# A decode kernel on one core: a hand-written program that closes its Tile context early, with its first load inside it, batch rows 16 partitions apart, and one DMA each for x and the output

## Chip, cores, metric

One core of a Trainium2 chip. The metric is the device time of one execution in microseconds (us). A profile gives the *span*, from the first to the last instruction of the program; the measured time is up to 1.9 us longer than the span. Clocks are the mean granted TensorE clock, as a share of full speed.

In the profiles PE is TensorE (matmuls), PEld its weight loads, DVE VectorE, ACT ScalarE, POOL GpSimd; SPq, ACTq and PEq are the instruction queues of SyncE, ScalarE and PE. A semaphore is a counter that one engine or DMA raises and another waits for. At an all-engine barrier every engine waits for all others. The Tile context is the scope in which the program is built; leaving it adds such barriers and instructions that the trace calls drains. wq, wo, w3 and w4 are weights; sg is the product of the attention branch and the gate.

## The reference

Grouped-query attention for one new token against a long cache, gated by a small MLP branch:

```python
B, Sq, D = 2, 1, 512;  Hq, Hkv, Sk, Dh = 32, 8, 32768, 128       # bf16
xn = layernorm(x)
q  = (xn @ wq)                                   # 32 heads; 4 heads share one K/V head
p  = softmax(q @ k_cache^T * Dh**-0.5);  o = p @ v_cache
s  = o @ wo
g  = silu(mlp_branch(xn, w3, w4))                # at S=1 the w1/w2 branch adds zero
return x + s * g
```

K and V are 2 x 8 x 32768 x 128 bf16 each, 268 MB together. Everything else is small.

## The kernel before

It is written by hand inside one `tc.tile_critical()`, with its own semaphores. SyncE issues all large loads in one queue, K and V of the 16 (batch, head) groups alternately; DVE transposes K, PE multiplies, ScalarE takes the exponential, PE multiplies by V. After the last group 128 short matmuls apply wo.

```python
with tc.tile_critical():
    ...
    k_wq = d_wq.after(sp.dma_start(out=wq_t[...], in_=A_wq...), 16)      # first load of the program
    k_w3 = ...;  k_w4 = ...;  load_k(0)
    ...
    for n in range(NQ):                                                  # x, four DMAs of two rows
        k_x = d_x.after(act.dma_start(out=x_bf[32*n:32*n+B, :], in_=A_x[:, 0, :]), 16)
    ...                                                                  # layernorms, q, the MLP branch
    wait(sp, k_h2)                                                       # frees the buffer of w3, w4
    load_v(0)
    for m in range(1, NG):
        sp.wait_ge(p_k, m);  load_k(m)
        sp.wait_ge(p_o, m);  load_v(m)
    for i, (g0, g1, c0, c1) in enumerate(WO_PARTS):                      # wo in 8 parts, last in the queue
        d_wo[i].after(sp.dma_start(out=wo3[...], in_=wos[...]), 16)
    ...
    with pe.Fori(0, NG): ...                                             # the 16 groups
    pe.wait_ge(s_r, NG)                                                  # last group's result
    for i, (g0, g1, c0, c1) in enumerate(WO_PARTS):
        wait(pe, (d_wo[i], 16))
        ...  pe.matmul(s_ps[32*n:32*n+B, :], lhsT=oXv[:, g, r, :], rhs=wo3[...])   # 128 in all
    ...                                                                  # two DVE operations: sg, out4
    for b, eng in ((0, sp), (1, act)):
        wait(eng, k)
        d_o[b].after(eng.dma_start(out=out[b, 0, :]..., in_=out4[b:QP:32, :]), 16)
    for b, eng in ((0, sp), (1, act)):
        wait(eng, (d_o[b], 16))
# leaving the context adds drains, two all-engine barriers and a clearing of semaphores
```

The softmax here doesn't subtract the row's maximum and nothing guards it: scores larger than these inputs give would overflow.

Of the kernel before, what the change touches and what calls it, by code (L numbers as in the profile page):

```python
# [7 lines left out]
F32 = mybir.dt.float32  # L8
BF16 = mybir.dt.bfloat16
I32 = mybir.dt.int32  # L10
# [5 lines left out]
RT = 16  # L16
VT = 4
T_BUFS = 4
PAD = 384
# [18 lines left out]
def wait(eng, *marks):  # L38
    for count, n in marks:
        if n > 0:  # L40
            eng.wait_ge(count.sem, n)
# [8 lines left out]
def kernel(  # L50
# [14 lines left out]
    nc = tc.nc  # L65
    pe, dve, act, pool, sp = nc.tensor, nc.vector, nc.scalar, nc.gpsimd, nc.sync
# [10 lines left out]
    NPART = 2  # L77
# [8 lines left out]
    QW = D // NQ  # L86
    QP = 32 * (NQ - 1) + B
    NU = KPT // VT
# [4 lines left out]

    pers = ctx.enter_context(tc.tile_pool(name="pers", bufs=1))
    psum = ctx.enter_context(tc.tile_pool(name="psum", bufs=1, space=bass.MemoryType.PSUM))

    pers.tile([128, PAD // 4], F32, name="pad")
    kbuf = pers.tile([128, 3 * SLOT], BF16, name="kbuf")
    vbuf = pers.tile([128, 2 * SLOT], BF16, name="vbuf")
    Ts = [pers.tile([128, RT * NB * 32], I32, name=f"T{i}") for i in range(T_BUFS)]  # L100
    eps_ = [pers.tile([128, RT * 32], BF16, name=f"ep{i}") for i in range(NPART)]
    pts = [pers.tile([128, NR, RT * rep], BF16, name=f"pt{i}") for i in range(NPART)]
    rss = [pers.tile([128, 1], F32, name=f"rs{i}") for i in range(NPART)]
    sms = [pers.tile([128, rep], F32, name=f"sm{i}") for i in range(NPART)]
    z = pers.tile([128, NB, 2, ZC], BF16, name="z")
    ob = pers.tile([128, VT * Dh], F32, name="ob")
    rec = pers.tile([128, rep], F32, name="rec")
    on = pers.tile([128, rep], BF16, name="on")
    xm = pers.tile([128, NQ, rep], F32, name="xm")
    oX = pers.tile([128, B * Hkv * NQ], BF16, name="oX")  # L110
    ident = pers.tile([128, 128], BF16, name="ident")
    ones_f = pers.tile([128, 128], F32, name="ones_f")
    sel = pers.tile([128, NB, 2, 4, 32], BF16, name="sel")
    sel_o = pers.tile([128, VT, rep], F32, name="sel_o")
    sel_h = pers.tile([128, rep], F32, name="sel_h")
    sel_r = pers.tile([128, NQ, 4, 32], BF16, name="sel_r")
    mask = pers.tile([128, NQ, rep], F32, name="mask")
    x_bf = pers.tile([128, D], BF16, name="x_bf")
    xf = pers.tile([128, D], F32, name="xf")
    xn = pers.tile([128, D], F32, name="xn")  # L120
    ln2 = pers.tile([128, D], F32, name="ln2")
    xn_bf = pers.tile([128, D], BF16, name="xn_bf")
    ln2_bf = pers.tile([128, D], BF16, name="ln2_bf")
    x4 = pers.tile([128, QW], F32, name="x4")
    xn4 = pers.tile([128, QW], F32, name="xn4")
    xT = pers.tile([128, 2 * DK, B], BF16, name="xT")
    q_sb = pers.tile([128, B, Hq], BF16, name="q_sb")
    qr = pers.tile([128, NB, 2, B * Hq], BF16, name="qr")
    hf = pers.tile([128, FK * B], F32, name="hf")
    x2 = pers.tile([128, FK * B], F32, name="x2")  # L130
    inner = pers.tile([128, FK * B], F32, name="inner")
    th = pers.tile([128, FK * B], F32, name="th")
    h_bf = pers.tile([128, FK * B], BF16, name="h_bf")
    t_f = pers.tile([128, QW], F32, name="t_f")
    sig = pers.tile([128, QW], F32, name="sig")
    g4 = pers.tile([128, QW], F32, name="g4")
    sg = pers.tile([128, QW], F32, name="sg")
    out4 = pers.tile([128, QW], BF16, name="out4")
    stats = [pers.tile([128, dve.BN_STATS_DIM], F32, name=f"stats{i}") for i in range(2)]
    mv = [pers.tile([128, dve.BN_AGGR_DIM], F32, name=f"mv{i}") for i in range(2)]  # L140
    rstd = [pers.tile([128, 1], F32, name=f"rstd{i}") for i in range(2)]

    banks = [psum.tile([128, 512], F32, name=f"bank{i}") for i in range(8)]
    sc = banks[0:2]
# [3 lines left out]
    xp = xp_b[:, 0:NQ * rep].rearrange("p (r h) -> p r h", h=rep)  # L148
    treg = treg_b[:, 0:DK * B].bitcast(BF16)
    qT_ps = sc[0][:, 0:Hq * B]  # L150
# [8 lines left out]

    with tc.tile_critical():  # L160
        d_x, d_wq, d_w3, d_w4 = (Count(nc, n) for n in ("d_x", "d_wq", "d_w3", "d_w4"))
        s_k = [nc.alloc_semaphore(f"s_k{i}") for i in range(NPART)]
        s_v = [nc.alloc_semaphore(f"s_v{i}") for i in range(NPART)]
        d_wo = [Count(nc, f"d_wo{i}") for i in range(len(WO_PARTS))]
        d_o = [Count(nc, f"d_o{i}") for i in range(B)]
        v_, p_, a_, g_ = (Count(nc, n) for n in ("v_", "p_", "a_", "g_"))
# [6 lines left out]
        def V(inst):  # L173
            return v_.after(inst)

        def P(inst):
            return p_.after(inst)
# [10 lines left out]

        wq_t = kbuf[:, 2 * SLOT:3 * SLOT]
        w34 = vbuf[:, 0:SLOT]  # L190
        wo3 = kbuf[:, 0:Hq * D].rearrange("p (g c) -> p g c", g=Hkv)

        k_wq = d_wq.after(sp.dma_start(out=wq_t[:, 0:DK * HD], in_=A_wq.rearrange("(p k) f -> p (k f)", k=DK)), 16)
        k_w3 = d_w3.after(sp.dma_start(out=w34[:, 0:W4O], in_=B_w3.rearrange("(p k) f -> p (k f)", k=DK)), 16)
# [25 lines left out]
        wait(act, k_x0)  # L220
        for n in range(NQ):
            k_x = d_x.after(act.dma_start(out=x_bf[32 * n:32 * n + B, :], in_=A_x[:, 0, :]), 16)

# [13 lines left out]
        V(dve.memset(o[:, :], 0.0))  # L237
        V(dve.memset(s_ps, 0.0))
        k_h0 = V(dve.memset(h2, 0.0))

# [23 lines left out]
        wait(dve, k_xn)  # L264
        k_xb = V(dve.tensor_copy(out=xn_bf[0:B, :], in_=xn[0:B, :]))
        k_l2 = layernorm(1, ln2, xn, k_xn)
        wait(dve, k_l2)
        k_lb = V(dve.tensor_copy(out=ln2_bf[0:B, :], in_=ln2[0:B, :]))

        wait(pool, k_n0, k_xn)  # L270
        for n in range(NQ):
            r0, r1, c0, c1 = 32 * n, 32 * n + B, n * QW, (n + 1) * QW
            wait(pool, (g_, g_.n))
            k = G(pool.tensor_copy(out=x4[r0:r1, :], in_=xf[r0:r1, c0:c1]))  # L274
            wait(pool, k)
            k_x4 = G(pool.tensor_copy(out=xn4[r0:r1, :], in_=xn[r0:r1, c0:c1]))

        wait(pe, k_id)
        for s, (src, k_src) in enumerate(((xn_bf, k_xb), (ln2_bf, k_lb))):
            wait(pe, k_src)  # L280
            for k in range(DK):
                c = (s * DK + k) * B
                k_tr = P(pe.transpose(out=treg[:, c:c + B], in_=src[0:B, k::DK], identity=ident[0:B, 0:B]))  # L283

# [27 lines left out]
        wait(dve, k_tr)  # L312
        k_xT = V(dve.tensor_copy(out=xT[:, :, :], in_=treg.rearrange("p (k b) -> p k b", b=B)))

        wq3 = wq_t[:, 0:DK * HD].rearrange("p (k f) -> p k f", k=DK)
        wait(pe, k_xT, k_wq)
        for h in range(Hq):
# [53 lines left out]
        wait(dve, k)  # L371
        k_hb = V(dve.tensor_mul(out=h_bf[:, :], in0=hf[:, :], in1=th[:, :]))
        wait(pe, k_h0, k_hb, k_w4)
        for f in range(FK):
            for n in range(NQ):
                i = pe.matmul(
                    h2[32 * n:32 * n + B, :], lhsT=h_bf[:, f * B:(f + 1) * B],
                    rhs=w4v[:, f, n * QW:(n + 1) * QW],
                    start=(f == 0), stop=(f == FK - 1), tile_position=(0, 32 * n),
                )  # L380
# [137 lines left out]

        oXv = oX[:, :].rearrange("p (b g r) -> p g r b", b=B, g=Hkv)
        pe.wait_ge(s_r, NG)  # L520
        for i, (g0, g1, c0, c1) in enumerate(WO_PARTS):
            wait(pe, (d_wo[i], 16))
            for g in range(g0, g1):
                for r in range(c0 // D, c1 // D):
                    for n in range(NQ):
                        c = r * D + n * QW
                        mm = pe.matmul(  # L527
                            s_ps[32 * n:32 * n + B, :], lhsT=oXv[:, g, r, :], rhs=wo3[:, g, c:c + QW],
                            start=(g == 0 and r == 0), stop=(g == Hkv - 1 and r == NQ - 1),
                            tile_position=(0, 32 * n),  # L530
                        )
# [4 lines left out]
        k = V(dve.tensor_tensor(out=out4[0:QP, :], in0=sg[0:QP, :], in1=x4[0:QP, :], op=ALU.add))  # L536
        for b, eng in ((0, sp), (1, act)):
            wait(eng, k)
            d_o[b].after(
                eng.dma_start(out=out[b, 0, :].rearrange("(n c) -> n c", c=QW), in_=out4[b:QP:32, :]), 16  # L540
            )
        for b, eng in ((0, sp), (1, act)):
            wait(eng, (d_o[b], 16))

# [29 lines left out]
```

## Time and profile before

657.5 us, median of three runs (657.25 to 657.61); span 655.9 us, clock 0.82.

| of the span | |
|---|---|
| start: first instruction to the first load packet | 1.98 us |
| stream: first load packet to the end of the last wo packet | 649.42 us |
| last wo packet to the first of the two last DVE operations | 0.61 us |
| those two, to the issue of the output DMA | 0.65 us |
| output issued by SyncE to its landing seen by SyncE | 1.95 us |
| from there to the last instruction (closing the context) | 1.29 us |

The rows come from the starts and ends of the trace's instructions and DMA packets and add up to the span. The page of the kernel before: parts 1 and 2 (busy time; the span in 40 slices, busy share in tenths) and the sum of part 3.

```profile
span 655.9 us, 7180 instructions
PE 391.5 (60%) x2716; PEld 168.8 (26%) x2748; DVE 337.2 (51%) x428; ACT 71.3 (11%) x167; POOL 5.6 (1%) x18
...
DMA  8999999999999999999999999999999999999996
...
q1 hardware_dynamic: 6744, 280.50, 99.0%
...
HBM read 280.50 MB, written 0.00 MB: 428 GB/s over the span
```

The DMA row is what to read: 90% or more in every slice but the first and the last. The SyncE queue (q1) carries the bytes and is never empty between its first and last packet. PE and DVE have slack; a time saved on them in the middle is worth nothing. What can be won without moving fewer bytes is the start and the tail.

The timeline of the kernel before, start and end (start us, duration us, engine, line, operation, tiles; in brackets the idle time before and what ended it; SPq and ACTq lines are DMA issues):

```profile
0.96 0.40 SPq L193 DMA_DIRECT2D kbuf<-in_A_wq_dram  x1
...
1.37 1.57 ACTq L222 DMA_DIRECT2D x_bf<-in_A_x_dram  x4
1.42 0.41 SPq L194 DMA_DIRECT2D vbuf<-in_B_w_dram  x1
...
13.53 0.43 DVE L242 CAST xf<-x_bf 128x512 f32<-128x512 bf16 x1 [11.31 <-DMA x_bf<-in_A_x_dram]
...
21.37 3.58 PE L319 MATMUL bank<-xT,kbuf 128*128 128x2 bf16 x128 [2.00 <-DVE xT L313]
...
32.40 0.33 SPq L202 DMA_DIRECT2D vbuf<-in_A_v_cache_dram  x1
...
641.77 1.90 PE L495 MATMUL bank<-vbuf,pt 128*16 128x512 bf16 x32 [1.89 <-PEq L46]
...
651.10 0.86 PE L527 MATMUL bank<-kbuf,oX 128*2 128x128 bf16 x16 [0.31 <-DMA kbuf<-in_A_wo_dram]
...
652.01 0.29 DVE L534 TENSOR_TENSOR sg<-bank,g 98x128 f32<-98x128 f32 x1 [4.69 <-PE bank L527]
652.34 0.29 DVE L536 TENSOR_TENSOR out<-sg,x 98x128 bf16<-98x128 f32 x1
652.65 0.66 SPq L540 DMA_DIRECT2D out_dram<-out  x1
652.66 0.60 ACTq L540 DMA_DIRECT2D out_dram<-out  x1
```

The first V load is issued at 32.40 us, while K of the first group keeps the queue busy to 42.1 us: the x chain in front of it has slack. At the end the wo matmuls wait for the last wo DMA, so the tail here is the DMA's. The span ends at 655.9 us, 3.2 us after the output is issued. The list of waits of the SyncE queue (who waited for what: us in total, times, longest) shows how much of this is the output's landing (1.3 us after its issue is over); the rest is the close:

```profile
SPq L160 <- DMA out_dram<-out: 1.3, 1, 1.3
SPq L558 <- PEq L558: 0.7, 1, 0.7
SPq L569 <- PEq L569: 0.5, 2, 0.4
```

### The profile page before, as it was taken

The numbers are of one execution on the slowest core, as the hardware profiler recorded it, in microseconds if no ns is written. First come the engines' busy times: TensorE is split into PE (matmuls) and PEld (weight loads), VectorE is DVE, ScalarE is ACT, GpSimd is POOL, SyncE is SP. The second block draws the span as 40 slices with busy tenths as digits, with TensorE's granted clock in tenths as the row PEclk, the third lists the DMA queues.
The fourth block names the chain that finished last, engine by engine and source line by source line (L and its number), as shares of the span: only waits on it lengthen the run. The fifth ranks groups of instructions, "written<-read, shape, count | busy, mean of one in ns | idle before, by whom it ended". The sixth has DMA issues, their size and how long they took to land. (4 is left out here: it accounts for less than half of the span.)

```text
span 655.9 us, 7180 instructions
## 1 busy us (share of the span) xinstructions
PE 391.5 (60%) x2716; PEld 168.8 (26%) x2748; DVE 337.2 (51%) x428; ACT 71.3 (11%) x167; POOL 5.6 (1%) x18
## 2 busy tenths in 40 slices
PE   0528295582838648293764829376382946728784
PEld 0513132221313223131331313223131322313323
DVE  2348092653809265290835629084471917448560
ACT  0110102001010200101020010202001020200100
POOL 1200000000000000000000000000000000000000
PEclk9999787686978868698786978779597876959898
DMA  8999999999999999999999999999999999999996
GB/s 365 436 441 448 441 408 440 440 444 440 404 440 444 444 420 428 440 444 444 400 448 440 444 444 400 448 436 448 440 404 444 440 444 416 432 440 418 444 420 263
DMA packets 6774, 280.59 MB, mean 428 GB/s; under 512 B 744, under 2 KB 1008, under 8 KB 2032
## 3 DMA queue, kind: packets, MB, share of 16 engines
q1 hardware_dynamic: 6744, 280.50, 99.0%
q8 instruction: 4, 0.07, 0.0%
q14 instruction: 2, 0.02, 0.0%
q10 hardware_dynamic: 24, 0.01, 0.0%
HBM read 280.50 MB, written 0.00 MB: 428 GB/s over the span
## 5 line engine op out<-in xcount | busy, mean ns | idle before, releaser
L477 PE MATMUL bank<-T,z 128*128 128x512 bf16 x992 | 274.2, 425 | 178.5 <-PEq L46 174.5
L434 DVE STREAM_TRANSPOSE T<-kbuf 128x1024 int32<-128x1024 int32 x256 | 290.9, 1206 | 131.2 <-DVEq L46 130.6
L477 PEld LDWEIGHTS bank<-T,z 128*128 128x128 bf16 x1024 | 98.4, 104 | 340.1 <-issue 262.5
L495 PE MATMUL bank<-vbuf,pt 128*16 128x512 bf16 x1024 | 73.2, 449 | 1.9 <-PEq L46 1.9
L413 ACT ACTIVATE ep<-bank 128x512 bf16<-128x512 f32 x32 | 19.1, 597 | 440.3 <-ACTq L46 440.3
L447 DVE RECIPROCAL rec<-bank 128x4 f32<-128x4 f32 x16 | 2.9, 182 | 118.2 <-DVEq L46 118.2
L495 PEld LDWEIGHTS bank<-vbuf,pt 128*16 128x16 bf16 x1024 | 27.8, 102 | 39.5 <-issue 21.7
L441 DVE STREAM_TRANSPOSE pt<-ep 128x512 bf16<-128x512 bf16 x32 | 22.1, 691 | 23.4 <-DVEq L46 23.4
L488 PE MATMUL bank<-sm,ones_f 128*128 128x4 f32 x64 | 9.3, 251 | 29.3 <-PEq L46 29.3
L506 PE MATMUL bank<-sel_o,ob 128*128 128x4 f32 x128 | 16.4, 252 | 13.8 <-PEq L46 13.8
L417 ACT COPY ob<-bank 128x512 f32<-128x512 f32 x16 | 9.4, 586 | 103.2 <-ACTq L46 103.2
L406 ACT ACT_TABLE_LOAD x16 | 20.5, 1283 | 0.3
L506 PEld LDWEIGHTS bank<-sel_o,ob 128*128 128x128 f32 x128 | 15.5, 191 | 18.2 <-issue 18.2
L488 PEld LDWEIGHTS bank<-sm,ones_f 128*128 128x128 f32 x64 | 8.3, 190 | 30.2 <-issue 30.2
L406 ACT COPY z<-qr 32x16 bf16 x64 | 12.9, 201 | 0.7
L512 PE MATMUL bank<-on,sel_r 128*128 128x4 bf16 x64 | 3.9, 165 | 12.6 <-PEq L46 12.6
L283 PE MATMUL bank<-ident,xn_bf 2*128 2x2 bf16 x4 | 0.3, 165 | 16.7 <-POOL x L274 16.7
L464 PE MATMUL bank<-ident 128*1 128x1 bf16 x64 | 8.3, 164 | 0.0
L464 PEld LDWEIGHTS bank<-ident 128*1 128x1 bf16 x64 | 4.0, 81 | 16.0 <-issue 14.2
L450 DVE TENSOR_TENSOR xm<-bank,mask 128x16 f32<-128x16 f32 x16 | 2.8, 174 | 8.6 <-DVEq L46 8.6
L512 PEld LDWEIGHTS bank<-on,sel_r 128*128 128x128 bf16 x64 | 2.9, 98 | 13.5 <-issue 13.5
L413 ACT ACTIVATION_READ_ACCUMULATOR ep<-bank 128x1 f32 x32 | 6.3, 198 | 0.2
(66 smaller groups left out, 58.8 us busy)
## 6 DMA issues: line engine op xcount, KB each, us to landing
kbuf<-in_A_k_cache_dram SPq DMA_DIRECT2D x2, 4096.0 KB, 22.7
vbuf<-in_A_v_cache_dram SPq DMA_DIRECT2D x2, 4096.0 KB, 25.6
kbuf<-in_A_wq_dram SPq DMA_DIRECT2D x1, 4096.0 KB, 12.2
vbuf<-in_B_w_dram SPq DMA_DIRECT2D x2, 1792.0 KB, 17.9
kbuf<-in_A_wo_dram SPq DMA_DIRECT2D x2, 1024.0 KB, 33.3
kbuf<-in_A_wo_dram SPq DMA_DIRECT2D x3, 512.0 KB, 35.7
kbuf<-in_A_wo_dram SPq DMA_DIRECT2D x1, 256.0 KB, 26.8
kbuf<-in_A_wo_dram SPq DMA_DIRECT2D x2, 128.0 KB, 15.6
```

Source lines behind the costliest of these rows:

```text
L406: i = act.copy(out=z[32 * j:32 * j + 32, :, :, c:c + rep], in_=qr[32 * j:32 * j + 32, :, :, bass.ds(m * rep, rep)],)
L413: act.activation(out=eps_[i][:, :], in_=sc[i][:, :], func=ACT.Exp, scale=inv_sqrt_dh, accum_out=rss[i][:, :]).then_inc(s_e, 1)
L417: act.copy(out=ob[:, :], in_=o[:, :]).then_inc(s_ob, 1)
L434: dve.transpose(out=Ts[(NR * i + r) % T_BUFS][:, :].rearrange("p (b t k) -> p t b k", b=NB, t=RT), in_=kt[:, r * W:(r + 1) * W].rearrange( ...
L441: dve.transpose(out=pts[h][:, :, :].rearrange("p r (t h) -> p t r h", h=rep), in_=eps_[i][:, :].rearrange("p (t r h) -> p t r h", r=NR, h= ...
L447: then(dve.reciprocal(out=rec[:, :], in_=S))
L464: pe.matmul(mark_ps, lhsT=ident[:, 0:1], rhs=ident[:, 0:1], start=True, stop=True).then_inc(sem, 1)
L477: mm = pe.matmul(sc[i][:, :], lhsT=z[:, nb, e, zc:zc + 128], rhs=Tb[:, nb, :, e], start=(r == 0 and nb == 0 and e == 0), stop=(r == NR - 1 ...
L488: pe.matmul(S, lhsT=ones_f[:, :], rhs=sms[h][:, :], start=(h == 0), stop=(h == NPART - 1))
L495: mm = pe.matmul(o[32 * j:32 * j + VT * rep, :], lhsT=pts[h][:, r, a * VT * rep:(a + 1) * VT * rep], rhs=vt[:, u * VT:(u + 1) * VT, :].rea ...
L506: mm = pe.matmul(oT, lhsT=ob[:, t * Dh:(t + 1) * Dh], rhs=sel_o[:, t, :], start=(t == 0), stop=(t == VT - 1))
L512: mm = pe.matmul(xp[:, r, :], lhsT=sel_r[:, r, :, :].rearrange("p j w -> p (j w)"), rhs=on[:, :], start=True, stop=True,)
```

## The change

The intent is to cut what the context adds at both ends: the buffers come from raw allocations, the context contains nothing but the first load (wq) and is closed before the rest of the program is written, so its barriers run behind wq's packets and nothing but one wait follows the output. And x and the output, four and two small DMAs, become one each: batch rows lie 16 partitions apart instead of next to each other, so that one regular pattern with step 16 reaches all eight (quarter, batch) rows. The price is 17 columns of PE weights for 2 and DVE operations on 113 rows for 98.

```diff
-    pers = ctx.enter_context(tc.tile_pool(name="pers", bufs=1))
-    kbuf = pers.tile([128, 3 * SLOT], BF16, name="kbuf")
+    kbuf = sbuf([128, 3 * SLOT], BF16, "kbuf")          # nc.alloc_sbuf_tensor; the same for all buffers
...
-    with tc.tile_critical():
+    first = sp.dma_start(out=wq_t[:, 0:DK * HD], in_=A_wq.rearrange("(p k) f -> p (k f)", k=DK))
+    first.then_inc(s_wq, 16)
+    tc.no_tile_sem_insts.add(first.ins.name)
+    tc.close()
+    tc.compile()
...
-        for n in range(NQ):
-            k_x = d_x.after(act.dma_start(out=x_bf[32 * n:32 * n + B, :], in_=A_x[:, 0, :]), 16)
+        k_x = d_x.after(act.dma_start(out=x_bf[0:QP:BS, :],
+                  in_=A_x[:, 0, :].unsqueeze(0).to_broadcast([NQ, B, D])), 16)      # BS = 16
...
-                            s_ps[32 * n:32 * n + B, :], lhsT=oXv[:, g, r, :], rhs=wo3[:, g, c:c + QW],
+                            s_ps[32 * n:32 * n + BW, :],                            # BW = 17
+                            lhsT=oX[:, g * NQ + r:g * NQ + r + BO + 1:BO // BS], rhs=wo3[:, g, c:c + QW],
...
-        for b, eng in ((0, sp), (1, act)):
-            d_o[b].after(eng.dma_start(out=out[b, 0, :]..., in_=out4[b:QP:32, :]), 16)
-        for b, eng in ((0, sp), (1, act)):
-            wait(eng, (d_o[b], 16))
+        sp.dma_start(out=out[:, 0, :].rearrange("b (n c) -> n b c", c=QW), in_=out4[0:QP:BS, :]
+        ).then_inc(s_out, 16)
+    sp.wait_ge(s_out, 16)
```

## The prediction

> **What bounds the kernel now.** The stream of loads. In the page's slices the 16 DMA engines are 90% busy or more from the second slice to the second last; 280.5 MB move at 428 GB/s. From the trace's DMA packets: the SyncE queue's first load packet starts at 1.98 us, the last wo packet ends at 651.40 us, and in between the queue is never empty. In the timeline each K and V load is issued some 7 to 12 us before the one ahead of it has landed. So PE (60% busy) and DVE (51%) have slack, and the time is 2.0 us of start + 649.4 us of stream + 4.5 us of tail.
>
> **What the change does.**
>
> 1. *Start.* Before, SyncE leaves the first barrier at 0.65 us, runs a NOP and a waiting branch, and issues wq at 0.96 us. After, wq is its first instruction: about 0.72 us, so the stream starts 0.24 us earlier. Two barriers now come after that issue. From those at the end of the old trace (about 0.4 us each), the w3 load, the memsets and the x load begin 0.3 to 0.8 us later: hidden behind wq's 10 us of packets.
>
> 2. *x load.* Four DMAs become one. In the old trace ScalarE's packets take turns with 32 KB packets of wq, one each 1.22 us per engine: four DMAs, each a data packet and a semaphore packet, last from 6.3 to 13.2 us. The Trainium skill ("DMA: Bandwidth & Descriptors", "Why a DMA increments its semaphore by 16 and not by 1") tells how many engines a copy uses: two for two rows (the trace agrees: two data packets a DMA), four for the new shape, so two data packets and one semaphore packet each. Estimate: x lands at 9 to 10 us instead of 13.2, the q matmuls start near 17 us (21.4), the first V load is issued near 28 us (32.4). Worth nothing: K0 keeps the queue busy to 42 us.
>
> 3. *Stream.* The same bytes, packet sizes and buffer addresses (compared in the two builds). PE weights of 17 columns for 2 and DVE operations on more rows cost the same by free size. Change 0 +-0.3 us.
>
> 4. *Tail.* After the last wo packet: four matmuls, two DVE operations (0.29 us each), output DMA. The two output DMAs are seen at 654.34 (ScalarE) and 654.61 us (SyncE). One DMA saves 0 to 0.25 us. Then the old kernel closes the context: drains, NOP, two barriers, a clearing of semaphores, from 654.61 to 655.90 us, all after the result has landed. After, a single wait ends it. Saves 1.25 us.
>
> On the critical path: 0.24 + 0.1 + 1.25 = 1.6 us. x load: nothing.
>
> **Prediction:** 655.9 us, 80% range 655.1 to 656.9 us. Chances: faster by over 2% 0.005, within 2% 0.99, slower 0.005.
>
> **What would show it.** Timeline: wq issued near 0.7 us; wait of xf for x ends at 9 to 10 us; first V load near 28 us; no gap in the SyncE queue, loads spaced 19.3 us; the last instruction near 654.3 us, under 0.2 us after the output DMA's semaphore.
>
> **What would make it wrong.** SyncE's drain after the wq issue waits until wq has landed: then w3 is issued near 13 us and the queue has a gap of 2 us (time near 657.7 us). Or the measured time holds parts outside the span (657.8 against 655.9 us in the profiled run) that grow as the barriers go. Or the stream's rate shifts by 0.2%.

## The result and the profile after

655.38 us (median of four runs, 655.07 to 656.12) against 657.39 us (four runs): ratio 0.9971, 95% interval 0.9954 to 0.9988. Ratios here are the mean time of one kernel's runs over that of the other's of the same rounds, so not quite the ratio of the quoted medians. That is 2.0 us less by the medians: clear of noise, but under the 2% from which a change counts as faster.

The timeline of the changed kernel, the lines that answer to those above:

```profile
0.73 0.39 SPq L164 DMA_DIRECT2D kbuf<-in_A_wq_dram  x1
1.91 0.33 SPq L202 DMA_DIRECT2D vbuf<-in_B_w_dram  x1
...
2.34 1.10 ACTq L230 DMA_DIRECT2D x_bf<-in_A_x_dram  x1
...
10.50 0.43 DVE L254 CAST xf<-x_bf 128x512 f32<-128x512 bf16 x1 [7.20 <-DMA x_bf<-in_A_x_dram]
...
18.44 3.57 PE L332 MATMUL bank<-xT,kbuf 128*128 128x2 bf16 x128 [2.09 <-DVE xT L325]
...
29.58 0.33 SPq L210 DMA_DIRECT2D vbuf<-in_A_v_cache_dram  x1
...
641.25 3.48 PE L515 MATMUL bank<-vbuf,pt 128*16 128x512 bf16 x32 [2.44 <-PEq L46]
...
648.43 3.32 PE L547 MATMUL bank<-kbuf,oX 128*17 128x128 bf16 x128 [0.79 <-DVE oX L472]
651.81 0.29 DVE L555 TENSOR_TENSOR sg<-bank,g 113x128 f32<-113x128 f32 x1 [3.43 <-PE bank L547]
652.14 0.29 DVE L557 TENSOR_TENSOR out<-sg,x 113x128 bf16<-113x128 f32 x1
652.46 0.69 SPq L559 DMA_DIRECT2D out_dram<-out  x1
```

and the waits of its SyncE queue:

```profile
SPq L562 <- DMA out_dram<-out: 1.0, 1, 1.0
SPq L577 <- PEq L577: 0.7, 1, 0.7
SPq L169 <- PEq L169: 0.4, 2, 0.3
```

What to see: wq is issued 0.22 us earlier, and the two barriers (L169) now stand between wq and w3 (L202, the second line). x arrives 3 us earlier and the first V load goes out 2.8 us earlier, for nothing, since K keeps the queue busy until 41.8 us. After the output's landing there is nothing: the last instruction is that wait, at 654.18 us.

One thing was not expected. In this profile the last 32 V matmuls take 3.48 us instead of 1.90, and then all 128 wo matmuls run without waiting for any wo DMA: the end is PE's, 0.94 us after the last wo packet, not 0.61. The granted clock tells why. Busy time by stretch for the kernel before (stretch, its length, then busy time and number of instructions of PE, PEld, DVE, ACT and POOL, clock, DMA share, GB/s):

```profile
634.00:641.00 7.00, 4.05 (x38) 1.59 (x37) 0.82 (x2) 0.69 (x2) 0.00 (x0) 0.76 0.90 387
641.00:648.00 7.00, 3.79 (x73) 2.63 (x77) 0.69 (x4) 0.58 (x1) 0.00 (x0) 0.93 1.02 418
```

and for the changed kernel:

```profile
634.00:641.00 7.00, 4.50 (x36) 1.91 (x36) 0.16 (x2) 0.00 (x0) 0.00 (x0) 0.52 0.95 406
641.00:648.00 7.00, 4.75 (x45) 2.33 (x45) 0.52 (x3) 0.59 (x1) 0.00 (x0) 0.74 1.02 418
```

0.52 and 0.74 of the clock for 0.76 and 0.93. The Trainium skill, "TensorE: Matmul & The Clock Gate", Part 1, describes a clock gate with a half and a full rate that is set by PE's recent activity in a free-running window of about 3.4 us. The clock records agree: the steps are 0.5 and 1.0, and the stretches near the end last 3.4 us or a multiple (10.2 us at half from 634.3 us in the changed kernel; 3.4 us at half from 636.8 us in the kernel before).

### The profile page after: what moved, and what is told of

Same layout as the page of the kernel before. It is cut to its first block, busy times and chain, and to the rows that moved or that the text cites. A ratio compares the mean times of both kernels' runs of the same rounds, so it can differ in the third digit from the quotient of the medians.

```text
span 654.2 us, 7191 instructions
## 1 busy us (share of the span) xinstructions
PE 404.3 (62%) x2748; PEld 169.8 (26%) x2748; DVE 337.5 (52%) x429; ACT 71.4 (11%) x167; POOL 5.0 (1%) x18
## 5 line engine op out<-in xcount | busy, mean ns | idle before, releaser
L497 PE MATMUL bank<-T,z 128*128 128x512 bf16 x1024 | 282.1, 424 | 168.4 <-PEq L46 163.6
L515 PE MATMUL bank<-vbuf,pt 128*16 128x512 bf16 x1024 | 77.3, 469 | 2.4 <-PEq L46 2.4
L508 PE MATMUL bank<-sm,ones_f 128*128 128x4 f32 x64 | 10.5, 270 | 29.3 <-PEq L46 29.3
```

The costliest lines, as they stand in the source:

```text
L497: mm = pe.matmul(sc[i][:, :], lhsT=z[:, nb, e, zc:zc + 128], rhs=Tb[:, nb, :, e], start=(r == 0 and nb == 0 and e == 0), stop=(r == NR - 1 ...
L508: pe.matmul(S, lhsT=ones_f[:, :], rhs=sms[h][:, :], start=(h == 0), stop=(h == NPART - 1))
L515: mm = pe.matmul(o[32 * j:32 * j + VT * rep, :], lhsT=pts[h][:, r, a * VT * rep:(a + 1) * VT * rep], rhs=vt[:, u * VT:(u + 1) * VT, :].rea ...
```

## The experiments

Theory A: the gain is the start and the close of the context; the data path is worth only the second output DMA. Theory B, a rival: it is the data path (x earlier, one DMA each). Later a second pair arose on a slow tail: C, it is the phase of the clock gate; D, the data path costs PE time there.

The terms of every trace, one profiled run each, in us. "Seen" is the end of the wait for the output.

| kernel | first packet | stream | last packet to sg | output issue to seen | seen to end | span |
|---|---|---|---|---|---|---|
| before | 1.98 | 649.42 | 0.61 | 1.95 | 1.29 | 655.9 |
| changed | 1.76 | 649.12 | 0.94 | 1.73 | 0.02 | 654.2 |
| after_again | 1.75 | 649.45 | 1.08 | 1.73 | 0.02 | 654.7 |
| ctx_only | 1.77 | 649.26 | 0.62 | 1.94 | 0.02 | 654.2 |
| dma_only | 1.97 | 649.07 | 2.13 | 1.73 | 1.29 | 656.8 |
| dma_again | 1.98 | 649.20 | 0.83 | 1.74 | 1.29 | 655.7 |
| wq_late | 2.40 | 649.12 | 0.62 | 1.74 | 0.02 | 654.5 |
| x_late12 | 1.75 | 649.16 | 1.48 | 1.73 | 0.02 | 654.8 |
| x_late40 | 1.75 | 666.14 | 0.67 | 1.73 | 0.02 | 671.0 |
| end_bar3 | 1.75 | 648.96 | 0.86 | 1.73 | 0.94 | 654.9 |
| hoist | 1.75 | 649.20 | 0.70 | 1.74 | 0.02 | 654.0 |
| hoist_again | 1.76 | 649.00 | 0.83 | 1.73 | 0.02 | 654.0 |
| dma_hoist | 1.99 | 648.90 | 0.87 | 1.74 | 1.29 | 655.4 |
| before_hoist | 1.99 | 649.04 | 0.71 | 1.95 | 1.29 | 655.6 |

Column by column: the start and "seen to end" follow the context handling alone; "output issue to seen" follows the number of output DMAs alone; the stream, the delayed-x run apart, varies by half a us without pattern; the third column, the tail, follows neither (see dma_again and wq_late).

### after_again: the changed kernel beside the next three

> The changed kernel once more, beside the runs below on the same chip. Expected by both theories: 1.6 to 2.0 us under the kernel before, wq issued at 0.73 us, last instruction within 0.1 us of the end of the wait for the output. Second question: in the trace already seen the last wo matmuls ran after the last wo packet had landed, with the PE clock at half for 10 us before. If that is the throttle's phase and not the change, another profile may show the last wo load waited for by PE, as before, and an end up to 0.9 us nearer to the last packet.

655.58 us (655.21 to 655.99, five runs) against 657.41 us (nine runs); ratio 0.9972, interval 0.9958 to 0.9985. The gain repeats. The tail again ended by PE, 1.08 us after the last packet, with another pattern of half-clock stretches (3.4 us each from 641.8 and 648.7 us). So the second question stays open here; the trace of wq_late, below, answers it.

### ctx_only: the context alone

```diff
 # the kernel before, with only this part of the change
+    first = sp.dma_start(out=wq_t[...], in_=A_wq...);  first.then_inc(s_wq, 16)
+    tc.close();  tc.compile()
-    with tc.tile_critical():
```

> The kernel before with the early close of the context, wq issued inside it and raw buffers; x by four DMAs, output by two, rows as before. Theory A (the gain is the context's start and close): 1.3 to 1.7 us under before; wq issued near 0.73 us, x landing at 14 to 15 us, first V load near 33 us, last instruction within 0.1 us of the second output DMA's landing. Theory B (the gain is the data path: x earlier, one DMA for each): within 0.3 us of before.

655.68 us (655.56 to 656.03, five runs), ratio 0.9977, interval 0.9964 to 0.9991. The means are 655.77 and 657.34 us: 1.57 us less (1.73 us by the medians). A holds, B falls. x was first used at 13.2 us (expected 14 to 15) and the first V load issued at 32.1 us, both only 0.3 us earlier than before, and that cost nothing.

### dma_only: the data path alone, and dma_again

```diff
 # the changed kernel, with the context handled as before
-    first = sp.dma_start(...);  tc.close();  tc.compile()
+    with tc.tile_critical():
+        k_wq = d_wq.after(sp.dma_start(...), 16)
```

> The other part alone: rows 16 apart, x and output one DMA each, inside the critical section with the context closed at the end as before. Theory A: 0 to 0.4 us under before (only the second output DMA is saved); x lands near 9.5 us, 1.2 us of drains and barriers still follow the output's landing. Theory B: 1.3 us or more under before.

658.13 us (657.25 to 658.97, five runs), ratio 1.0011, interval 0.9997 to 1.0024. B falls again, but A's expectation was missed too: not 0 to 0.4 us under but 0.7 us over by the medians. The output DMA's 0.22 us is there (1.73 us to "seen" for 1.95); the tail lost it. The timeline of dma_only:

```profile
641.42 3.59 PE L508 MATMUL bank<-vbuf,pt 128*16 128x512 bf16 x32 [2.61 <-PEq L46]
...
645.87 1.84 PE L519 MATMUL bank<-sel_o,ob 128*128 128x4 f32 x8 [0.86 <-PEq L46]
...
649.53 3.60 PE L540 MATMUL bank<-kbuf,oX 128*17 128x128 bf16 x128 [0.79 <-DVE oX L465]
653.18 0.29 DVE L548 TENSOR_TENSOR sg<-bank,g 113x128 f32<-113x128 f32 x1 [3.70 <-PE bank L540]
```

and its stretches, with the clock at 0.50 from 641 us on:

```profile
634.00:641.00 7.00, 3.17 (x36) 1.34 (x36) 0.82 (x2) 0.53 (x2) 0.00 (x0) 0.73 0.92 395
641.00:648.00 7.00, 5.43 (x41) 2.97 (x41) 0.14 (x1) 0.59 (x1) 0.00 (x0) 0.50 1.02 419
648.00:653.00 5.00, 3.71 (x132) 3.51 (x132) 0.55 (x4) 0.00 (x0) 0.00 (x0) 0.50 0.41 150
```

The five runs order themselves by mean clock: 657.25 us at 0.820, 657.69 at 0.814, 658.13 at 0.810, 658.72 and 658.97 at 0.806. The same program went again on another chip:

> The data path alone once more: it came out 0.7 us over the kernel before (median) where 0 to 0.4 us under was expected. Its trace has the PE clock at half from 637 us to the end, and the last wo matmuls end 2.1 us after the last wo packet (0.55 us in the kernel before). Theory C (chance of the throttle's phase): single times spread over 1.5 us again, the fastest at or under the kernel before, and the slower ones have the lower mean clock. Theory D (the change in the data path itself costs time in the tail, by 17 columns of weights for 2): slower in every run, whatever the clock of the tail.

657.25 us (657.17 to 657.58, five runs), ratio 0.9994, interval 0.9980 to 1.0008. The expected spread did not show, but D, slower in every run, falls: four of the five were under the median of the kernel before (657.53 us) and the fifth 0.05 us over it, and its trace ends 0.83 us after the last packet instead of 2.13. So the slow runs of dma_only are not its code. By C they are the clock, and the trace shows that for the run it holds. The mean clock of a whole run says less: dma_again has 657.25 us at 0.811 and 657.58 us at 0.820; what counts is where the half-clock stretches fall. Why four of five were slow in the first series is not known.

The fourteen traces together say more. Within each, every change in the record of the clock lies on one grid of 3.41 us, to 0.01 us; how the grid lies to the program differs from trace to trace. Where the last 32 V matmuls begin 1.5 to 2.2 us into a step of this grid, they run at full clock and take 1.90 us: before, ctx_only, before_hoist, wq_late, x_late40. In the other nine traces they begin 0.2 to 0.9 or 2.7 to 3.3 us into a step, meet a stretch at half clock and take 2.96 to 3.59 us. That fits C. Two of the five, wq_late and x_late40, carry the 17 columns. What stays untested is whether the changed data path makes an unfavourable place of the grid more likely: all three traces with 2 columns are among the five, and only two of the eleven with 17.

### wq_late: the start term alone

```diff
-    first = sp.dma_start(...wq...)
     tc.close();  tc.compile()
+    first = sp.dma_start(...wq...)
```

> The changed kernel with the wq load issued after the early close, so behind the two barriers. Theory A, with the stream gapless: wq is issued near 1.5 us (the two barriers without the DMA ahead of SyncE's drain), 0.8 us later than in the change, and every load and the end come 0.8 us later: 0.8 us over the changed kernel, 0.8 to 1.2 us under before. If early slack can be taken up later (rival), the time is that of the changed kernel.

wq was issued at 1.38 us, so 0.65 us later, not 0.8, and the first packet came at 2.40 us for 1.75, with the stream as long as in the changed kernel's first trace (649.12 us). So the start moves the end of the stream, as A says, as far as one trace can tell: the streams themselves differ by half a us, and the delay of x_late40, below, shows it more sharply. The time, 655.87 us (655.74 to 657.72; ratio 0.9986, interval 0.9972 to 1.0), is 0.3 us over after_again by medians and 0.7 us by means, because one run of five had a clock of 0.805 and took 657.72 us. The trace resolves the start itself; the times do not, nor do the spans (654.5 us here, 654.7 for after_again): against after_again the stream was 0.33 us shorter and the tail 0.46 us.

That tail answers the second question of after_again. With the same 17 columns the last 32 V matmuls ran at full clock (1.90 us), the last wo matmuls waited for their DMA again, and sg started 0.62 us after the last packet, as in the kernel before (0.61). x_late40 shows the same (1.90 and 0.67 us). The timeline of wq_late:

```profile
641.89 1.90 PE L514 MATMUL bank<-vbuf,pt 128*16 128x512 bf16 x32 [1.81 <-PEq L46]
...
651.21 0.87 PE L546 MATMUL bank<-kbuf,oX 128*17 128x128 bf16 x16 [0.29 <-DMA kbuf<-in_A_wo_dram]
652.13 0.29 DVE L554 TENSOR_TENSOR sg<-bank,g 113x128 f32<-113x128 f32 x1 [4.69 <-PE bank L546]
```

So the 17 columns alone do not make a tail bound by PE; in all six unhoisted traces that have one, the last V matmuls met a half clock.

### x_late12 and x_late40: what the x chain is worth

```diff
         wait(dve, k_x)
+        for _ in range(12):                      # x_late40: 40
+            wait(dve, V(dve.memset(ln2[:, :], 0.0)))
         k_xf = V(dve.tensor_copy(out=xf[:, :], in_=x_bf[:, :]))
```

> The changed kernel with 12 dependent fills of an idle buffer (about 0.5 us each) on DVE between the landing of x and its first use. The first V load should be issued about 6 us later, near 36 us, still before K0 ends on the queue at 42 us. Theory A (the x chain has some 11 us of slack): time that of the changed kernel within 0.4 us. Rival (the x chain is on the critical path): 6 us slower.

> The same with 40 fills: about 21 us, first V load near 51 us, a gap in the queue of about 9 us after K0. Theory A: time 8 to 11 us over the changed kernel (1.2 to 1.7%), that is the delay less the slack, and nothing of it made up later. If the later loads could catch up: within 2 us.

x_late12: 655.91 us (655.69 to 656.11), ratio 0.9970, interval 0.9955 to 0.9985: as the changed kernel, although the first V load was issued at 37.67 us, later than in the kernel before. x_late40: 672.81 us (672.38 to 673.31), 16.9 us more than x_late12. The size was missed: a fill with its wait took about 0.66 us ((55.81 - 29.58) / 40 from the two timelines), not 0.5, so the first V load went out at 55.81 us. Its first packet came at 56.78 us instead of 39.94, 16.84 us later, and the stream grew by 16.9 us over that of the other runs. The stretches of x_late40 show the hole (the second last number is the DMA share):

```profile
30.00:40.00 10.00, 0.10 (x3) 0.13 (x4) 7.79 (x19) 0.20 (x1) 0.49 (x2) 1.00 0.97 420
40.00:57.00 17.00, 9.39 (x252) 8.82 (x251) 6.65 (x31) 3.76 (x6) 2.86 (x7) 1.00 0.13 44
57.00:70.00 13.00, 10.65 (x42) 4.38 (x44) 12.90 (x12) 2.43 (x7) 0.00 (x0) 1.00 1.00 429
```

The hole was not made up later; as long as there was none (x_late12), the x chain was free. So the earlier x of the change is worth nothing.

### end_bar3: barriers behind the result

```diff
     sp.wait_ge(s_out, 16)
+    nc.all_engine_barrier();  nc.all_engine_barrier();  nc.all_engine_barrier()
```

> The changed kernel with three all-engine barriers after the wait for the output. By the old trace one barrier lasts 0.3 to 0.5 us. Theory A: 0.9 to 1.4 us over the changed kernel, in the measured time as in the span. Rival (what lies behind the result is hidden in the time's own tail outside the span): no change in the time, only in the span.

656.75 us (656.57 to 658.13), ratio 0.9989, interval 0.9975 to 1.0002: 1.2 us over after_again by medians (another chip; by the ratios to the kernel before 1.1 us). The rival falls. But the span grew by only 0.92 us (0.94 for 0.02 us from "seen" to the end). The rest is outside the span: time less span is 1.75 to 1.83 us in these five runs and 1.28 to 1.40 us in those of after_again. That holds for all runs: 1.81 us in the mean of the 27 runs of the kernel before listed with the experiments and 1.83 us in 25 runs of the others that end in barriers, 1.36 us in 37 runs of those that end in SyncE's wait.

### hoist, before_hoist, dma_hoist, hoist_again: PE's wo work taken out of the tail

Of the 128 wo matmuls 112 belong to heads that were done before the last group. The last group is taken out of PE's loop, and they are put into its waits:

```diff
-        with pe.Fori(0, NG): <group>
-        pe.wait_ge(s_r, NG)
-        for i in range(8): wo_part(i)
+        with pe.Fori(0, NG - 1): <group>
+        pe.wait_ge(s_r, NG - 1)
+        <group, with wo_part(0) ahead of its wait for ob and wo_part(1) ahead of its wait for on>
+        for i in (2, 3, 4): wo_part(i)
+        pe.wait_ge(s_r, NG)
+        for i in (5, 6, 7): wo_part(i)
```

> A new version: the changed kernel with the PE's last group taken out of the loop, and the wo matmuls that do not need the last group's result (parts 0 to 4 of 8, 112 of 128 matmuls) put into its waits, as their data lands. If the end is bound by PE at a throttled clock in some runs: those runs gain up to 0.9 us, the median 0.3 to 0.7 us under the changed kernel, and the last wo load is what the last matmuls wait for, whatever the clock. If the end is bound by the last wo packet anyway: same as the changed kernel within 0.2 us.

655.37 us (655.15 to 655.52, five runs), ratio 0.9962, interval 0.9948 to 0.9975. The timeline of hoist:

```profile
644.48 0.98 PE L497 MATMUL bank<-kbuf,oX 128*17 128x128 bf16 x32
...
646.50 0.63 PE L497 MATMUL bank<-kbuf,oX 128*17 128x128 bf16 x32
...
650.74 0.86 PE L497 MATMUL bank<-kbuf,oX 128*17 128x128 bf16 x16 [0.18 <-DMA kbuf<-in_A_wo_dram]
651.65 0.29 DVE L571 TENSOR_TENSOR sg<-bank,g 113x128 f32<-113x128 f32 x1 [3.32 <-PE bank L497]
```

The last matmuls wait for the last wo DMA again, although the clock is at half from 648.6 us to the end. Whether the expected 0.3 to 0.7 us came, the times don't settle: see hoist_again.

> The same move in the kernel before. Where the last wo packet ends its run, nothing is to be had: 0 to 0.5 us under before in the median, its slower runs (those with a low clock) gone. If the tail's PE work is a cost in every run of before: 0.7 us or more.

657.26 us (657.23 to 657.60), ratio 0.9995, interval 0.9981 to 1.0008. As expected: nothing in the median beyond 0.3 us, but no run like the 658.29 and 658.91 us that the kernel before had in the same rounds.

> The data path alone, with the 112 wo matmuls that do not need the last group put into the last group's waits. Theory C: they are out of the throttled tail, so 1.0 us or more under dma_again in the median, under the kernel before by 0 to 0.6 us, and a spread of under 0.8 us; last matmul 0.5 to 0.8 us after the last wo packet. Theory D: within 0.3 us of dma_again.

657.21 us (657.15 to 657.29), ratio 0.9993, interval 0.9979 to 1.0007. It was expected 1.0 us under dma_again and was 0.04 us under, because dma_again had no slow runs this time. This pair alone therefore decides nothing between C and D. The spread, 0.14 us, is as C wants it; against dma_only of the other chip it is 0.9 us less.

> The best version so far once more, beside the others: 2.0 to 2.6 us under the kernel before (it was 0.9962 of it), and 1.3 to 1.6 us under dma_hoist, which is the start and the close of the context again, now free of the throttle's noise.

655.47 us (655.31 to 655.76), ratio 0.9967, interval 0.9953 to 0.9981: 2.06 us under the kernel before, and 1.74 us under dma_hoist. That is more than the 1.3 to 1.6 us expected: the spans of the two profiled runs differ by 1.4 us, as expected, and I had left out what lies outside the span.

The ten runs of the hoisted version have a median of 655.45 us and a range of 655.15 to 655.76; the nine of the changed kernel 655.52 us, 655.07 to 656.12. The version beats the kernel before. Against the changed kernel nothing is shown: the two never ran in the same rounds, the medians differ by 0.1 us, the ratios to the kernel before by what would be 0.3 to 0.6 us, and their intervals are about 0.9 us to each side. Only the upper end seems trimmed.

## Why the prediction was right

It was right: 655.38 us lies within 655.1 to 656.9, and the 1.6 us forecast became 2.0 us. Point by point:

- *What bounds the kernel.* Right. The stream takes 648.9 to 649.5 us in every trace but that of x_late40, and a hole of 16.8 us in it cost 16.9 us.
- *Start, 0.24 us.* 0.22 us (first packet 1.98 to 1.76 us). SyncE's drain behind the wq issue did not wait for wq to land: it took 0.12 us. The barriers delayed x by 0.97 us (issue 1.37 to 2.34), not 0.3 to 0.8.
- *x load, worth nothing.* Right in worth, shown by x_late12 and ctx_only. The times were off by 0.5 to 1.6 us: first use at 10.5 us, q matmuls at 18.4, first V load at 29.6, for 9 to 10, 17 and 28. The mechanism held: the Trainium skill's rule of how many engines a copy uses ("DMA: Bandwidth & Descriptors", "Why a DMA increments its semaphore by 16 and not by 1") gave four engines, and the trace has on ScalarE's queue eight 1 KB packets and four semaphore packets for x, each engine's 1.25 us apart, between the large ones.
- *Stream, 0 +- 0.3 us.* In the first pair of traces it was 0.31 us shorter. Its values over all kernels lie within 0.6 us, with no order in them, so I take it for noise. The wider weights and rows cost nothing that the traces resolve: 1.66 and 1.68 us for the 56 matmuls on h_bf, 0.29 us for sg on 98 and on 113 rows.
- *Output DMA, 0 to 0.25 us.* 0.22 us, the same in every trace that has one output DMA.
- *Close, 1.25 us.* 1.27 us in the span (1.29 to 0.02).
- *The term that was mis-sized.* "On the critical path: 0.24 + 0.1 + 1.25 = 1.6 us" leaves out the part of the time outside the span. I had named it only as a danger, as something that might grow. It shrank by 0.45 us (1.81 to 1.36 us), and end_bar3 shows that barriers at the end bring it back. What it is made of no run shows. The Trainium skill, "Runtime: NRT & Kernel Launch", "The launch sequence", lists about 1.5 us for a wait for all engines after the kernel; that the engines that finish early get part of such work done ahead of SyncE is a guess from this.
- *What the prediction did not see.* The tail is not the DMA's alone. In this run PE, at a half clock, gave 0.33 us back (0.94 for 0.61 us).

So for the profiled pair the span is shorter by 0.22 (start) + 0.31 (stream) - 0.33 (tail) + 0.22 (output) + 1.27 (close) = 1.69 us (655.9 to 654.2), and the time by 0.45 us or so more. That the changes of stream and tail, both forecast as none, cancel here to 0.02 us is luck.

Open: what sets how the clock's grid lies to the program; why one series of dma_only was slow in four of five runs and another in none; and what the time outside the span consists of.

## What to carry to other kernels

When one DMA queue is busy from end to end, first prove it by the packets, then look only at what lies before its first packet and after its last: here every term of the gain sat there, and 3 us won on the chain of x were worth nothing. Do not end a kernel in barriers that nothing needs: they cost their own length in the span, and here another 0.45 us behind it. If short PE work ends the kernel, keep what does not depend on the last group out of the tail, because the clock may be at half just then; judge such small effects by the terms of the traces, and by spreads as well as medians.

## What the Trainium skill lacked or had wrong

- "Runtime: NRT & Kernel Launch": nothing on how the way a program ends moves the time outside its span. Here 1.36 us where only SyncE (or SyncE and ScalarE) waits last, 1.81 us where an all-engine barrier comes last.
- No page that I read prices an all-engine barrier that a program itself issues, or says if a drain on the issuing engine waits for its DMAs: three barriers took 0.92 us, and SyncE's drain 0.12 us while its 4 MB load had 11 us to go.
- "DMA: Bandwidth & Descriptors" gives about 2.0 us fixed for a DMA on the GpSimd path; for a 2 KB output issued by SyncE the runs show 1.73 us from the start of the issue to the end of the wait, and 1.95 us when ScalarE issued another at the same time. It says that queues interleave on the engines ("Issuing engines are not separate DMA queues") but not what a small copy pays for it: here 1.25 us a packet and engine, so four 2 KB copies took until 13.2 us and one 8 KB copy until 10.2 us.
- "TensorE: Matmul & The Clock Gate" says that the window's phase makes the start of a run variable and its cost small. Here the place of the half-clock stretches also decided the end: 0.61 to 2.13 us from the last packet to sg, a difference of 1.5 us where the whole gain is 2 us.
